# Splitting a chunk's output products by halves of the array's rows, and giving them a slot and banks of their own

## The chip, the cores and the metric

The kernel runs on one core of one Trainium2 chip. The metric is device time in microseconds (us), the median over runs of the whole program, from launch to the last store. Engines are named as in the profile: PE is the matrix engine (PEld its weight loads), DVE the vector engine, ACT the scalar engine, POOL the general one, and SP issues most DMAs.

## What is computed

A gated linear attention (a recurrence over 768 tokens, 4 batches, 8 heads of 48), whose output, laid side by side over the heads, goes through a feed-forward block of 384 to 2048 to 384 with SiLU:

```python
for t in range(S):                       # attention, state is 48 x 48 per head
    state = alpha[:, :, t, :, None] * state + einsum('bhd,bhe->bhde', k[:, :, t], v[:, :, t])
    y[:, :, t] = einsum('bhd,bhde->bhe', q[:, :, t], state)
x = y.transpose(0, 2, 1, 3).reshape(B * S, H * D)          # 3072 x 384
h = x @ w_in                                               # 384 x 2048
out = (h / (1 + exp(-h))) @ w_out                          # 2048 x 384
```

All of it is in 32-bit floats.

## The kernel before

**Chunks.** The tokens are cut into 24 chunks of C = 128 (chunk n is tokens of batch n % 4; CH = 64 is half a chunk). With scaled keys `kp` and queries `qp` (one tile holds four pairs of heads, a pair's two heads in rows 0 to 47 and 64 to 111), a chunk's attention is three kinds of product on PE:

- `scores`: keys times queries, a 128 x 128 matrix per head, of which the part with key after query is zero. ACT copies it from the accumulator banks (`ps_a`) to the tile `g`, and POOL's `affine_select` clears the wrong triangle.
- `values`: y, the chunk's output, is the sum of what comes from inside the chunk (`vn` times `g`, 16 products) and what comes from earlier chunks (the state `st` times `qp`, 12 products). Each fills 32 columns of the array, so four stand side by side (4 x 32 columns), and streams 128 tokens. All sum up in one bank, `py`; one ACT copy brings it to `xt`, the input of the feed-forward block.
- `states`: 16 products of 48 tokens add the chunk's keys and values to the state (DVE adds them).

From the ninth chunk on (n >= NA = 8) the scores of a chunk are already made in quarters (64 x 64), and the tokens of heads 4 to 7 stand with their two halves swapped, in `kp`, in `g` and in `v` alike, so that the four quarters of the array are busy at once.

**Feed-forward.** For groups of four chunks it runs as fast matrix multiplication (fewer products, more sums on DVE): `enter` makes the hidden layer (`ps_m`, 128 x 256 products), `leave` the output (`ps_o`, 128 x 192 products). Both are cut into pieces of some 2.6 us of PE time; a table of due times (`fill`) puts pieces between the attention's stages.

**Order.** `for step in range(5, STEPS)` has four slots a step. From step 8 on: slot 0 `land` and `scores` of the chunk before, slot 1 `products` (DVE: decays and `kp`), slot 2 `quotient` (DVE: `p`, then `qp`), slot 3 `values`, `states` and `flip` of the chunk before; after each slot `fill` runs the pieces that are due. On PE, the order is kept as written; on DVE, ACT and POOL a scheduler orders what is not marked (`settled`, `keep_in_program_order`), but once built the order of every engine is fixed, and each engine runs its queue strictly in that order. `least` is a chunk's total decay; ACT multiplies the state by it at the end of `scores`.

The pool `ps_a` has three banks, given out in rotation: two to `scores`, one to `values`, one to `states`.

Of the kernel before, what the change touches and what calls it, by code (L numbers as in the profile page):

```python
# [14 lines left out]
ALU = mybir.AluOpType  # L15
# [341 lines left out]
def quotients(  # L357
# [19 lines left out]
    nc = tc.nc  # L377
    dve, act, gps = nc.vector, nc.scalar, nc.gpsimd

    late = {}  # L380
# [7 lines left out]
    def settled(ins):  # L388

        return tc.keep_in_program_order(ins) if stated[0] else ins  # L390
# [55 lines left out]
    def ps_attn(n=C):  # L446
        return ps_a.tile([128, 512], F32, name="ps_a").rearrange("p (j c) -> p j c", c=n)
# [67 lines left out]
    def load_v(n):  # L515
        c = ctxs.setdefault(n, dict(zip(("ci", "b"), divmod(n, B))))
        x = v[c["b"], :, c["ci"] * C : c["ci"] * C + C, :].transpose([1, 0, 2])
        t = c["v"] = vns[n % NV]
        if n < NA:
            settled(nc.sync.dma_start(t[:, :, 0:D], x))  # L520
            return
        nc.sync.dma_start(t[:, 0 : H // 2, 0:D], x[:, 0 : H // 2])
        for e in range(2):
            nc.sync.dma_start(t[CH * e : CH * e + CH, H // 2 :, 0:D], x[CH - CH * e : C - CH * e, H // 2 :])

    wide = moe_w_in.dtype != F32
    pieces_in = [(t, c) for c in range(0, DF, 512) for t in range(NKT)]
# [238 lines left out]
    def products(n):  # L766

        if "ps" not in ctxs[n]:
            bring(n)
        c = ctxs[n]  # L770
        sg = seg[0 if late else n % 2]
        ps = c.pop("ps")
        end = NP * W
        u = upool.tile([128, end + 1], F32, name="u")
        settled(dve.tensor_tensor_scan(u[:, end - 1 :: -1], sg[:, end:0:-1], one[:, end:0:-1],  # L775
                                       0.0, ALU.mult, ALU.add))

        settled(dve.tensor_single_scalar(least[:, n, :], u[:, 0:end:W], 2.0**-64, ALU.max))  # L778
        kp = c["kp"] = turns(kps, n) if n < NA else kps[0]
        ut = tokens(u)  # L780
        if n >= NA:
            ps["k"] = late["turn"].tile([128, NP, C], F32, name="turn")
            turned(c["k"], ps["k"])
            load(n + 1, "k")
        if n < NA:
            settled(dve.tensor_tensor(kp, ps["k"], ut, ALU.mult))  # L786
            quotient(n, sg, ps["q"])
            return
        j = NP // 2
        dve.tensor_tensor(kp[:, 0:j], ps["k"][:, 0:j], ut[:, 0:j], ALU.mult)  # L790
        k, ut = [x[:, j:].rearrange("p j (e c) -> p j e c", e=2) for x in (ps["k"], ut)]
        dve.tensor_tensor(kp[:, j:].rearrange("p j (e c) -> p j e c", e=2)[:, :, ::-1], k, ut, ALU.mult)
        c["sg"] = sg

    def quotient(n, sg=None, q=None):
# [38 lines left out]
    def scores(n):  # L834
        c = ctxs[n]
        ci, b = c["ci"], c["b"]
        ps = [ps_attn() for _ in range(2)]

        for j in (0, 2, 1, 3):
            for e in range(2 if n >= NA else 1):
                for u in range(2):
                    r = slice(64 * u, 64 * u + D)
                    at = slice(CH * e, CH * e + CH) if n >= NA else slice(0, C)
                    t = slice(CH * (e ^ j // 2) if n >= NA else 0, C)
                    pe.matmul(ps[u][at, j, t], lhsT=c["kp"][r, j, at], rhs=c["qp"][r, j, t],
                              start=True, stop=True)
        if n == 1:

            room = gpool.tile([128, 4, 2, TB], F32, name="g").rearrange("p a b n -> p (a b n)")
            c["room"] = room[:, 2 * NP * C :]
        g = (room[:, 0 : 2 * NP * C] if n == 1 else decayed).rearrange(
            "p (u j c) -> p u j c", u=2, j=NP)
        swapped = decayed.rearrange("p (o u j c) -> p o u j c", o=2, u=2, j=NP // 2)
        c["g"] = (lambda u, j: g[:, u, j, :]) if n < NA else (
            lambda u, j: swapped[:, j // 2, u, j % 2, :])
        for u in range(2 if n < NA else 0):
            settled(act.copy(g[:, u], ps[u]))  # L859
            gps.affine_select(g[:, u], g[:, u], pattern=[[0, NP], [1, C]], compare_op=ALU.is_ge,  # L860
                              fill=0.0, base=0, channel_multiplier=-1)
        if n >= NA:
            ps = [x.rearrange("p (o j) c -> p o j c", o=2) for x in ps]
            for u in range(2):
                act.copy(swapped[:, :, u, :, CH:], ps[u][:, :, :, CH:])  # L865
            for r, o in earlier:
                for u in range(2):
                    act.copy(swapped[r, o, u, :, 0:CH], ps[u][r, o, :, 0:CH])
# [7 lines left out]
        if ci > 0:  # L876
            s = st[b].rearrange("p j u e -> p j (u e)")
            for j in range(NP):
                mul = act.mul(s[:, j], s[:, j], least[:, n, j : j + 1])
                if late or n == 6:  # L880
                    tc.keep_in_program_order(mul)

# [15 lines left out]
    def values(n):  # L898

        c = ctxs[n]  # L900
        ci, b, g, qp = c["ci"], c["b"], c.pop("g"), c["qp"]
        vn = c["v"].rearrange("p (j u) d -> p j (u d)", u=2)
        s = st[b].rearrange("p j u e -> p j (u e)")
        py = ps_attn()
        todo = [(3 * j + i, vn[:, j, at : at + 32], g(u, j))
                for j in range(NP) for i, at, u in ((0, 0, 0), (1, 32, 0), (2, 80, 1))]
        todo += [(3 * j + 1, vn[:, j, 48:80], g(1, j)) for j in range(NP)]
        if ci == 0:
            at = (0, 32, 48, 80)
            todo = [(3 * j + (i + 1) // 2, vn[:, j, at[i] : at[i] + 32], g(i // 2, j))  # L910
                    for j, i in ((0, 0), (0, 1), (2, 0), (1, 0), (1, 1), (3, 0), (3, 1), (2, 1),
                                 (0, 3), (0, 2), (1, 2), (3, 3), (1, 3), (2, 3), (2, 2), (3, 2))]
        if ci > 0:
            todo += [(3 * j + i, s[:, j, 32 * i : 32 * i + 32], qp[:, j, :])
                     for j in range(NP) for i in range(3)]
        for i, (at, w, x) in enumerate(todo):
            t, at = divmod(at, 4)
            pe.matmul(py[32 * at : 32 * at + 32, t, :], lhsT=w, rhs=x, start=(i < 4),
                      stop=(i >= len(todo) - 4), skip_group_check=True)
        half, e = divmod(n, 2)  # L920
        if e == 0:
            xts[half] = xtp.tile([128, NKT, TB], F32, name="xt")
        settled(act.copy(xts[half][:, :, e * C : (e + 1) * C], py[:, 0:NKT]))  # L923
    def states(n):
        c = ctxs.pop(n)
        ci, b, vn = c["ci"], c["b"], c["v"]
# [322 lines left out]
    def go_on():  # L1249

        nonlocal done
        next(pieces[done][0], None)
        done += 1
# [34 lines left out]
    def start():  # L1288
# [64 lines left out]
        stated.pop()  # L1353
        stated.append(False)

    start()
    for step in range(5, STEPS):
        stages = [[(scores, 1)], [(products, 0)], [(values, 1)], [(states, 1)]]
        if step < NA:
            stages = stages[0:2] + [stages[2] + stages[3], []]  # L1360
        elif step >= NA:
            stages = [[(land, 1), (scores, 1)], [(products, 0)], [(quotient, 0)],
                      [(values, 1), (states, 1), (flip, 0)]]
        for slot, group in enumerate(stages):
            for stage, lag in group:
                n = step - lag
                if not 0 <= n < NT:
# [8 lines left out]
            if step * SLOTS + slot == (NA + 1) * SLOTS - 1:  # L1376
                x = decayed.rearrange("p (o i c) -> p o i c", o=2, c=C)
                for r, o in later:
                    gps.memset(x[r, o, :, 0:CH], 0.0)
# [85 lines left out]
```

## Time and profile before

| what | number |
| --- | --- |
| median of 3 runs | 550.11 us (549.88 to 550.41) |
| the profiled execution's own time | 549.8 us |
| its span, first to last instruction | 548.1 us |
| PE busy / PEld / DVE / ACT / POOL | 98% / 90% / 79% / 39% / 14% of the span |
| share of the chain that ended last | PE 96%, of it `ps_m` 45%, `ps_o` 38%, `ps_a` 14% (two lines of code) |
| clock granted to PE | 0.999 of full |

How to read it: a 32-bit product of the code shows as two MATMUL rows of the trace (and two LDWEIGHTS rows), so the 16 + 12 + 16 products of `values` and `states` are 88 rows. MATMUL rows overlap: a row lasts from its start until its result is written, and the next one starts long before that. What counts is the distance between starts. `128*32` in a row is the part of the array in use, rows by columns; `128x128` is what it streams. In the rows of DVE, too, the next one starts some 0.08 us before the last has ended.

### The profile page before, as it was taken

What the parts mean: (1) busy time and instruction counts of PE and PEld (TensorE: products, weight loads), DVE (VectorE), ACT (ScalarE), POOL (GpSimd) and SP (SyncE); (2) the same over time, 40 slices, a digit from 0 to 9 for tenths busy, and PEclk for the clock granted to TensorE, in tenths of its full rate; (3) what the DMA queues carried; (4) which work ended last, traced back from release to release, by engine and by line L of the source; (5) the groups of instructions that cost most, each with busy time, mean ns of one, the idle gap of its engine ahead of it and who ended that gap; (6) DMA issues with size and microseconds to landing.
All of it is one profiled execution on the core that took longest, in us unless ns stands there. A gap on an engine that the chain in (4) does not pass through costs nothing.

```text
span 548.1 us, 12704 instructions
## 1 busy us (share of the span) xinstructions
PE 538.7 (98%) x5069; PEld 493.1 (90%) x5069; DVE 432.8 (79%) x753; ACT 216.3 (39%) x490; POOL 79.4 (14%) x146
## 2 busy tenths in 40 slices
PE   8899999999999999999999999999999999999996
PEld 8788888998999899899999999998998999999996
DVE  5999789986979799996998986998884796944421
ACT  3655554223333334444444354253264342432200
POOL 4111001131212201111121021021121000001000
PEclk9999999999999999999999999999999999999999
DMA  9999861355445434445455653716742144500001
GB/s 213 301 203 248 220 188 33 94 147 139 111 120 134 122 84 119 122 138 159 123 132 146 186 134 98 212 28 167 192 126 85 54 129 148 166 9 19 12 22 35
DMA packets 99219, 70.12 MB, mean 128 GB/s; under 512 B 56272, under 2 KB 88656, under 8 KB 99152
## 3 DMA queue, kind: packets, MB, share of 16 engines
q1 hardware_dynamic: 97232, 65.30, 46.0%
q0 software_dynamic: 1920, 3.93, 2.1%
q8 instruction: 41, 0.67, 0.5%
q14 instruction: 26, 0.21, 0.1%
HBM read 61.34 MB, written 7.86 MB: 126 GB/s over the span
## 4 chain that ended last, share of the span: by engine, by line
PE 96%; DVE 1%; issue 1%; POOL 0%; ACT 0%; DVEq 0%; ACTq 0%; POOLq 0%
PE ps_m L395 45%; PE ps_o L395 38%; PE ps_a L395 12%; PE ps_a L399 2%; DVE p L805 0%; DVE u L775 0%; PE ps_o L399 0%; POOL g L860 0%; DVE p L812 0%; DVE kp L786 0%; ACT xt L923 0%; ACT g L859 0%; ACT al L764 0%; DVE least L778 0%; ACT o L1130 0%
## 5 line engine op out<-in xcount | busy, mean ns | idle before, releaser
L395 PE MATMUL ps_o<-w_out,g 128*128 128x192 f32 x720 | 125.6, 328 | 0.0
L395 PEld LDWEIGHTS ps_o<-w_out,g 128*128 128x128 f32 x720 | 117.8, 190 | 2.7 <-issue 0.4
L395 PE MATMUL ps_m<-xt,w_in 128*128 128x256 f32 x480 | 111.6, 381 | 0.5 <-ACT xt L923 0.5
L395 PEld LDWEIGHTS ps_m<-xt,w_in 128*128 128x128 f32 x480 | 89.9, 190 | 12.7 <-ACT xt L923 0.8
L395 PE MATMUL ps_o<-wt,g 128*128 128x192 f32 x528 | 91.4, 326 | 0.0
L395 PEld LDWEIGHTS ps_o<-wt,g 128*128 128x128 f32 x528 | 87.3, 190 | 1.7 <-DVE o L1132 0.3
L395 PE MATMUL ps_m<-xc,w_in 128*128 128x256 f32 x288 | 70.6, 381 | 0.0
L1123 DVE TENSOR_TENSOR g<-g 128x512 f32<-128x512 f32 x72 | 49.6, 702 | 14.6 <-PE ps_o L395 12.2
L872 POOL TENSOR_SCALAR_AFFINE_SELECT g<-g 64x256 f32<-64x256 f32 x64 | 36.0, 563 | 165.3 <-ACT g L865 162.1
L395 PEld LDWEIGHTS ps_m<-xc,w_in 128*128 128x128 f32 x288 | 53.7, 190 | 6.7
L1015 ACT ACTIVATE g<-g 128x1024 f32<-128x1024 f32 x32 | 33.2, 1057 | 55.5 <-DVE g L1018 55.5
L1010 ACT COPY g<-ps_m 128x512 f32<-128x512 f32 x64 | 37.0, 587 | 36.7 <-PE ps_m L395 36.6
L395 PE MATMUL ps_m<-xc,wx 128*128 128x256 f32 x192 | 50.1, 383 | 0.0
L1135 POOL DMA_DIRECT2D out_dram<-o x40 | 22.1, 552 | 169.9 <-ACT o L1130 74.9
L1018 DVE TENSOR_TENSOR g<-ps_m,g 128x512 f32<-128x512 f32 x56 | 37.5, 684 | 10.9 <-PE ps_m L395 10.5
L395 PEld LDWEIGHTS ps_m<-xc,wx 128*128 128x128 f32 x192 | 35.2, 190 | 4.1 <-issue 0.4
L775 DVE TENSOR_TENSOR_SCAN u<-al,one 128x516 f32<-128x516 f32 x24 | 29.7, 1236 | 7.0 <-ACT al L764 6.6
L983 ACT ACTIVATE g<-ps_m 128x512 f32<-128x512 f32 x32 | 19.0, 597 | 33.2 <-PE ps_m L395 32.9
L805 DVE TENSOR_TENSOR_SCAN p<-al,inv 128x516 f32<-128x516 f32 x24 | 29.8, 1243 | 2.0 <-PE ps_a L395 1.1
L728 DVE TENSOR_REDUCE seen<-bits 128x1 f32<-128x512 int32 (+1 forms) x33 | 26.2, 820 | 6.0 <-DMA bits<-in_moe_w_in_dram 6.0
L1010 ACT COPY part<-ps_m 128x512 f32<-128x512 f32 x32 | 18.9, 590 | 30.4 <-PE ps_m L395 20.4
L1132 DVE TENSOR_TENSOR o<-ps_o,u 128x192 f32<-128x192 f32 x21 | 7.4, 353 | 26.9 <-PE ps_o L395 11.8
(142 smaller groups left out, 681.4 us busy)
## 6 DMA issues: line engine op xcount, KB each, us to landing
bits<-in_moe_w_in_dram SPq DMA_DIRECT2D x24, 512.0 KB, 5.1
bits<-in_moe_w_out_dram SPq DMA_DIRECT2D x16, 384.0 KB, 3.9
at<-in_alpha_dram SPq DMA_DIRECT2D x64, 96.0 KB, 2.6
kt<-in_k_dram SPq DMA_DIRECT2D x64, 96.0 KB, 2.7
qt<-in_q_dram SPq DMA_DIRECT2D x64, 96.0 KB, 2.8
bits<-in_alpha_dram SPq DMA_DIRECT2D x9, 512.0 KB, 4.0
out_dram<-o POOLq DMA_DIRECT2D x40, 96.0 KB, 2.2
flips<-turn SPq DMA_DIRECT2D x12, 256.0 KB, 2.4
```

What stands on the lines that cost most here:

```text
L395: in_order(nc.tensor.matmul(*args, **kw))
L399: in_order(nc.tensor.transpose(*args))
L728: dve.tensor_reduce(seen[kind][which][:, i : i + 1], x, axis=AX, op=op, apply_absolute_value=True))
L775: settled(dve.tensor_tensor_scan(u[:, end - 1 :: -1], sg[:, end:0:-1], one[:, end:0:-1], 0.0, ALU.mult, ALU.add))
L805: settled(dve.tensor_tensor_scan(p[:, 0:end], sg[:, 0:end], iv[:, 0:end], 0.0, ALU.mult, ALU.add))
L872: gps.affine_select(x, x, pattern=[[0, NP], [1, CH]], compare_op=ALU.is_ge, fill=0.0, base=0, channel_multiplier=-1)
L983: settled(act.activation(gts[grp, h, pair][:, i : i + 2, q % 2, :], ps, AF.Silu))
L1010: act.copy(to, ps)
L1015: return act.activation(x, x, AF.Silu)
L1018: dve.tensor_tensor(to, a, b, op)
L1123: dve.tensor_tensor(cells(grp, h, pair, *to), cells(grp, h, pair, *x), cells(grp, h, pair, *y), ALU.subtract)
L1135: (gps if grp < NG - 1 else nc.sync).dma_start(out[r : r + C, c * HO : (c + 1) * HO], o)
```

## The change

It is in the chunks from the ninth on.

- Swapped halves: instead of heads 4 to 7, the heads of every odd pair are swapped (2, 3, 6, 7). `load_v` needs six DMAs a chunk for that in place of three; `products` writes `kp` in two instructions as before, by even and odd pairs.
- y goes to three banks of `ps_a` (one for each 128 of its 384 rows), with accumulation flags of their own for each block of 32.
- `outer`, the state's share of y, is taken out of `values` and runs in slot 2, a slot sooner. Four of its products use all 128 rows of the array; the other eight, which touch one head each, use 64 rows, so that eight tiles of 64 x 32 stand side by side.
- `inner`, the chunk's own share, stays in slot 3. The later 64 tokens see all keys: 16 products of 128 rows, 64 tokens. The earlier 64 tokens see only the first 64 keys: 16 products of 64 rows and 64 tokens, eight side by side. In place of 28 products of 128 tokens a chunk has 44.
- `decay`, the state's multiplication by `least`, goes from the end of `scores` to slot 2, after `outer` of the chunk before and `quotient`.
- ACT copies y in three pieces (128 x 128) in place of one, and copies one column of a bank after `outer`.
- `apart`: one feed-forward piece is taken ahead and stands between `inner` and `states`.
- Two POOL memsets of `g` fall away.

```diff
-        nc.sync.dma_start(t[:, 0 : H // 2, 0:D], x[:, 0 : H // 2])
-        for e in range(2):
-            nc.sync.dma_start(t[CH * e : CH * e + CH, H // 2 :, 0:D], x[CH - CH * e : C - CH * e, H // 2 :])
+        to, x = [y.rearrange("p (j o u) d -> p o j u d", o=2, u=2) for y in (t[:, :, 0:D], x)]
+        for j in range(NP // 2):
+            nc.sync.dma_start(to[:, 0, j], x[:, 0, j])
+            for e in range(2):
+                nc.sync.dma_start(to[CH * e : CH * e + CH, 1, j], x[CH - CH * e : C - CH * e, 1, j])
...
+    def decay(n):
+        s = st[ctxs[n]["b"]].rearrange("p j u e -> p j (u e)")
+        for j in range(NP):
+            mul = act.mul(s[:, j], s[:, j], least[:, n, j : j + 1])
...
+    def add_y(n, j, i, half, w, x, t):
+        c = ctxs[n]
+        bank, at = divmod(3 * j + i, 4)
+        r = (low, high, slice(0, C))[half]
+        pe.matmul(c["y"][bank][32 * at : 32 * at + 32, t], lhsT=w[r], rhs=x[r, t],
+                  start=(j, i) not in c["begun"], stop=True, skip_group_check=True)
+        c["begun"].add((j, i))
+
+    def outer(n):
+        c = ctxs[n]
+        c["y"], c["begun"] = [ps_attn()[:, 0] for _ in range(NKT)], set()
+        s = st[c["b"]].rearrange("p j u e -> p j (u e)")
+        def add(j, i, half):
+            add_y(n, j, i, half, s[:, j, 32 * i : 32 * i + 32], c["qp"][:, j, :], slice(0, C))
+        for j in range(NP):
+            add(j, 1, 2)
+        for j in range(NP):
+            add(j, 0, 0)
+            add((j + 2) % NP, 2, 1)
+        act.copy(table, c["y"][1][:, 0:1])
+
+    def inner(n):
+        c = ctxs[n]
+        g, vn = c.pop("g"), c["v"].rearrange("p (j u) d -> p j (u d)", u=2)
+        def add(j, i, u, half, t):
+            at = (0, 32 + 16 * u, 80)[i]
+            add_y(n, j, i, half, vn[:, j, at : at + 32], g(u, j), t)
+        parts = ((0, 0), (1, 0), (2, 1)), ((1, 1),)
+        for part in parts:
+            for j in range(NP):
+                for i, u in part:
+                    add(j, i, u, 2, high)
+        for even, odd in (((0, 0, 0), (1, 1, 0)), ((0, 1, 0), (3, 0, 0)), ((2, 0, 0), (3, 1, 0)),
+                          ((2, 1, 0), (1, 0, 0)), ((2, 2, 1), (1, 1, 1)), ((0, 1, 1), (1, 2, 1)),
+                          ((0, 2, 1), (3, 1, 1)), ((2, 1, 1), (3, 2, 1))):
+            add(*even, 0, low)
+            add(*odd, 1, low)
+        x = x_of(n)
+        for t in range(NKT):
+            act.copy(x[:, t], c["y"][t])
...
+    def apart(n):
+        at = work_at[done]
+        while done < len(pieces) and pieces[done][2] <= bridged and work_at[done] == at:
+            go_on()
...
-            stages = [[(land, 1), (scores, 1)], [(products, 0)], [(quotient, 0)],
-                      [(values, 1), (states, 1), (flip, 0)]]
+            stages = [[(land, 1), (scores, 1)], [(products, 0)],
+                      [(outer, 1), (quotient, 0), (decay, 0)],
+                      [(values, 1), (apart, 1), (states, 1), (flip, 0)]]
```

The order on the engines moves at three places. Line numbers are those of each kernel: L739, L790, L792, L812, L1106 and L1123 of before are L741, L791, L793, L813, L1168 and L1185 after.

PE, the end of chunk 9 (counted from 0): `vn` times `g` and `st` times `p` are y, `vn` times `kn` are the states, `p` times `kp` the next chunk's scores, `ps_m` and `ps_o` feed-forward pieces. Before:

```order
L395 MATMUL ps_m<-xt,w_in 128x256 x6
L395 MATMUL ps_o<-wt,g 128x192 x8
L395 MATMUL ps_a<-g,vn_142 32x128 x16
L395 MATMUL ps_a<-p_166,st_178 32x128 x12
L395 MATMUL ps_a<-vn_142,kn 32x48 x16
L395 MATMUL ps_m<-xt,w_in 128x256 x6
L395 MATMUL ps_a<-p,kp_164 64x128 x2
```

And now:

```order
L395 MATMUL ps_m<-xt,w_in 128x256 x6
L395 MATMUL ps_a<-p_166,st_178 32x128 x12
L395 MATMUL ps_o<-wt,g 128x192 x8
L395 MATMUL ps_a<-g,vn_142 32x64 x32
L395 MATMUL ps_m<-xt,w_in 128x256 x6
L395 MATMUL ps_a<-vn_142,kn 32x48 x16
L395 MATMUL ps_a<-p,kp_164 64x128 x2
```

Small products stood at two places of a chunk, and now stand at three: the state's share alone, the chunk's own share alone, and the states with the next scores right behind them.

DVE, the query product of chunk 9 (L812, later L813: it writes `p`, which that chunk's scores read). `turn` is the transposed keys or queries; L1106 (L1168) and L1123 (L1185) are sums and differences inside `g`, the feed-forward's hidden layer. Before:

```order
L739 STREAM_TRANSPOSE turn<-kt 128x4x4x32
L790 TENSOR_TENSOR kp_164<-turn,u 128x256
L792 TENSOR_TENSOR kp_164<-turn,u 128x2x2x64
L739 STREAM_TRANSPOSE turn<-qt 128x4x4x32
L812 TENSOR_TENSOR p_166<-turn,p_166 128x4x128
L1106 TENSOR_TENSOR g<-g 128x2x2x128
```

And now:

```order
L741 STREAM_TRANSPOSE turn<-kt 128x4x4x32
L1185 TENSOR_TENSOR g<-g 128x2x2x128
L791 TENSOR_TENSOR kp_164<-turn,u 128x2x128
L793 TENSOR_TENSOR kp_164<-turn,u 128x2x2x64
L1185 TENSOR_TENSOR g<-g 128x2x2x128
L741 STREAM_TRANSPOSE turn<-qt 128x4x4x32
L605 TENSOR_TENSOR wx<-w_in 128x256
L813 TENSOR_TENSOR p_166<-turn,p_166 128x4x128
```

The two differences of `leave` (L1185) now stand ahead of the query product. They overwrite the `g` that the piece `ps_o<-w_out,g x8` reads, the piece that `apart` put between `inner` and `states` of chunk 8.

DVE, the query product of chunk 12, where a group of four chunks ends and the sums `xc` over its y (`xt`) are made for the next `enter`. Before:

```order
L739 STREAM_TRANSPOSE turn<-kt 128x4x4x32
L790 TENSOR_TENSOR kp_164<-turn,u 128x256
L792 TENSOR_TENSOR kp_164<-turn,u 128x2x2x64
L601 TENSOR_TENSOR xc<-xt 128x256 x2
L739 STREAM_TRANSPOSE turn<-qt 128x4x4x32
L1106 TENSOR_TENSOR g<-g 128x2x2x128
L812 TENSOR_TENSOR p<-turn,p 128x4x128
```

And now:

```order
L603 TENSOR_TENSOR xc<-xt 128x256
L741 STREAM_TRANSPOSE turn<-kt 128x4x4x32
L603 TENSOR_TENSOR xc<-xt,xc 128x256
L791 TENSOR_TENSOR kp_164<-turn,u 128x2x128
L793 TENSOR_TENSOR kp_164<-turn,u 128x2x2x64
L603 TENSOR_TENSOR xc<-xt 128x256 x2
L741 STREAM_TRANSPOSE turn<-qt 128x4x4x32
L608 SCALAR_TENSOR_TENSOR xc<-xt,xc 128x256
L813 TENSOR_TENSOR p<-turn,p 128x4x128
```

The sums over `xt`, which wait for the copy of y, now begin ahead of the transposed keys, and five of them stand ahead of the query product.

More of the change, by code (lines that the diff above doesn't have):

```diff
@@ L788, in products @@
             return
[L789 to L792, printed above, removed]
+        dve.tensor_tensor(kp[:, 0::2], ps["k"][:, 0::2], ut[:, 0::2], ALU.mult)
+        k, ut = [x[:, 1::2].rearrange("p j (e c) -> p j e c", e=2) for x in (ps["k"], ut)]
+        dve.tensor_tensor(kp[:, 1::2].rearrange("p j (e c) -> p j e c", e=2)[:, :, ::-1], k, ut, ALU.mult)
         c["sg"] = sg
@@ L837, in scores @@
         ps = [ps_attn() for _ in range(2)]
-        for j in (0, 2, 1, 3):
+        for j in range(NP):
             for e in range(2 if n >= NA else 1):
@@ L845, in scores @@
                     at = slice(CH * e, CH * e + CH) if n >= NA else slice(0, C)
[L846 removed]
+                    t = slice(CH * (e ^ j % 2) if n >= NA else 0, C)
                     pe.matmul(ps[u][at, j, t], lhsT=c["kp"][r, j, at], rhs=c["qp"][r, j, t],
@@ L856, in scores @@
         c["g"] = (lambda u, j: g[:, u, j, :]) if n < NA else (
-            lambda u, j: swapped[:, j // 2, u, j % 2, :])
+            lambda u, j: swapped[:, j % 2, u, j // 2, :])
         for u in range(2 if n < NA else 0):
@@ L862, in scores @@
         if n >= NA:
-            ps = [x.rearrange("p (o j) c -> p o j c", o=2) for x in ps]
+            ps = [x.rearrange("p (j o) c -> p o j c", o=2) for x in ps]
             for u in range(2):
@@ L875, in scores @@
             back(n)
[L876 to L881, printed above, removed]
+        if 0 < ci and n < NA:
+            decay(n)
+    def decay(n):
+        s = st[ctxs[n]["b"]].rearrange("p j u e -> p j (u e)")
+        for j in range(NP):
+            mul = act.mul(s[:, j], s[:, j], least[:, n, j : j + 1])
+            if late or n == 6:
+                tc.keep_in_program_order(mul)
     def back(n):
@@ L900, in values @@
         c = ctxs[n]
+        if n >= NA:
+            return inner(n)
         ci, b, g, qp = c["ci"], c["b"], c.pop("g"), c["qp"]
@@ L919, in values, with x_of @@
                       stop=(i >= len(todo) - 4), skip_group_check=True)
+        settled(act.copy(x_of(n), py[:, 0:NKT]))
+    def x_of(n):
         half, e = divmod(n, 2)
@@ L922, in values @@
             xts[half] = xtp.tile([128, NKT, TB], F32, name="xt")
-        settled(act.copy(xts[half][:, :, e * C : (e + 1) * C], py[:, 0:NKT]))
+        return xts[half][:, :, e * C : (e + 1) * C]
+    def add_y(n, j, i, half, w, x, t):
[25 more added lines that the diff above has]
+        for part in parts:
+            for j in range(NP):
+                for i, u in part:
[8 more added lines that the diff above has]
+            act.copy(x[:, t], c["y"][t])
     def states(n):
@@ L1366, in quotients @@
                 n = step - lag
-                if not 0 <= n < NT:
+                if not 0 <= n < NT or n < NA and stage in (outer, decay, apart):
                     continue
@@ L1375, in quotients @@
                     load_v(n + NV)
[L1376 to L1379, printed above, removed]
             fill(step, slot)
```

## The prediction

> **What bounds the kernel now.** I read the page's busy times first, then its chain, then the chain in order of time over one step, then PE's timeline inside one burst of small products.
>
> ```profile
> PE 538.7 (98%) x5069; PEld 493.1 (90%) x5069; DVE 432.8 (79%) x753; ACT 216.3 (39%) x490; POOL 79.4 (14%) x146
> PEclk9999999999999999999999999999999999999999
> PE 96%; DVE 1%; issue 1%; POOL 0%; ACT 0%; DVEq 0%; ACTq 0%; POOLq 0%
> ```
>
> PE carries the chain at full clock, so every 0.1 us added to PE's queue is 0.1 us of time. The chain over the step that ends chunk 12 (start, us, what):
>
> ```profile
> 204.01 2.01 PE ps_a L395 x88
> 206.02 2.79 PE ps_m L395 x12
> 208.81 0.81 PE ps_a L395 x24
> 209.63 2.81 PE ps_o L395 x16
> 212.44 2.59 PE ps_m L395 x12
> 215.03 2.60 PE ps_o L395 x16
> ...
> 224.75 2.01 PE ps_a L395 x88
> ```
>
> A step is 20.7 us without a gap. The piece behind a burst of small products takes 2.79 or 2.81 us, the same piece elsewhere 2.59 or 2.60: **leaving a burst costs 0.20**. PE's rows of the burst (start, us from first start to last end):
>
> ```profile
> 203.94 1.08 PE L395 MATMUL ps_a<-g,vn 128*32 128x128 f32 x32
> 204.84 0.84 PE L395 MATMUL ps_a<-p,st 128*32 128x128 f32 x24
> 205.50 0.52 PE L395 MATMUL ps_a<-vn,kn 128*32 128x48 f32 x32
> ...
> 205.95 1.13 PE L395 MATMUL ps_m<-xc,wx 128*128 128x256 f32 x4
> ```
>
> From 204.84 to 205.50 are 24 rows, four side by side, six rounds: 0.109 a round of 128 tokens. The 32 rows of 48 tokens are eight rounds; the last of them starts at 205.82 (below), which makes 0.043 a round. So a round is some 0.0025 plus 0.00083 a token, and one of 64 tokens, which the trace lacks, 0.056 (estimate between these two rows). Entering costs too:
>
> ```profile
> 203.69 0.33 PE L395 MATMUL ps_o<-wt,g 128*128 128x192 f32 x1
> 203.94 0.32 PE L395 MATMUL ps_a<-g,vn 128*32 128x128 f32 x4
> ...
> 205.82 0.21 PE L395 MATMUL ps_a<-vn,kn 128*32 128x48 f32 x1
> 205.95 0.48 PE L395 MATMUL ps_m<-xc,wx 128*128 128x256 f32 x1
> ```
>
> A piece of 2.60 has 16 rows of 192, 0.162 each, so the first row here is through at 203.85: 0.09 of nothing, and then 0.03 for the first weights of 32 columns (a quarter of the 0.11 that is left of the 0.20 on leaving): **0.12 to enter**. On leaving, the last row is through at 205.86, again 0.09 earlier. The four starts of a round lie within 0.02 (0.32 for all four against 0.30 for one), 7 ns apart.
>
> Is it a switch between sizes as such, or only to and from the full array? Rows where only the array's rows change, and where one small size follows another:
>
> ```profile
> 77.21 0.28 PE L395 MATMUL ps_a<-p,kp 48*128 48x128 f32 x2
> 77.42 0.33 PE L399 MATMUL ps_a<-ident,kp 128*128 128x128 f32 x1
> ...
> 15.36 0.27 PE L395 MATMUL ps_a<-p,kp 48*128 48x128 f32 x1
> 15.56 0.32 PE L395 MATMUL ps_a<-g,vn 128*32 128x128 f32 x4
> ```
>
> Rows of 128 tokens take 0.109, so the gaps are 77.42 − 77.32 and 15.56 − 15.47: 0.09 to 0.10 both times. Every switch of size costs that.
>
> **The change, part by part.**
>
> *Streaming.* Before, y takes 28 products, 56 rows, 14 rounds of 0.109: 1.53 us. Now `outer` has two rounds of 128 rows and two of eight 64-row tiles (4 × 0.109 = 0.44), `inner` eight and four rounds of 64 tokens (12 × 0.056 = 0.67). That saves **0.42** a chunk. Eight tiles at once the trace doesn't show; four of 64 x 64 it does, and there row halves run together:
>
> ```profile
> 208.74 0.33 PE L395 MATMUL ps_a<-p,kp 48*64 48x128 f32 x4
> ```
>
> The cost of the 64-row rounds lies between one turn and two; I take one, since both halves start within this row's 0.02.
>
> *Switches.* Before, a chunk's first burst costs 0.12 + 0.20, and the scores their own. Now `outer` enters (0.12), changes to 64 rows (0.12) and leaves (0.20); `inner` does the same; the states enter (0.12) and the scores follow them at no more than they paid before. That is 1.00 against 0.32: **+0.68** for 12 chunks. The last four have no states: 0.88 − 0.32 = **+0.56**. The last tile of a group starts 0.02 late with four tiles, 7 × 7 ns = 0.05 with eight: 0.16 now against 0.02, **+0.14** (+0.12 in the last four).
> PE's queue thus grows by 12 × (0.68 + 0.14 − 0.42) + 4 × (0.56 + 0.12 − 0.42) = **5.8 us**.
>
> The page "TensorEngine Tiling (Array Packing)" of the Trainium skill, section Key Properties, says that changing the tiling mode drains the array, while another tile of the same mode does not. The four switches above agree with it; by it the switch from 128 to 64 rows inside `outer` and `inner`, which no row shows with 32 columns, costs a drain too, and without it the sum would be 16 × 2 × 0.12 = 3.9 us less.
>
> *The scores' wait for DVE.* DVE is strict in order, and its new order puts work that waits for late things ahead of the query product. Durations (mean ns after the busy time):
>
> ```profile
> L1123 DVE TENSOR_TENSOR g<-g 128x512 f32<-128x512 f32 x72 | 49.6, 702 | 14.6 <-PE ps_o L395 12.2 <-PE ps_m L395 2.3
> L739 DVE STREAM_TRANSPOSE turn<-qt 128x512 f32<-128x512 f32 x16 | 17.9, 1118 | 0.3
> L601 DVE TENSOR_TENSOR xc<-xt 128x256 f32<-128x256 f32 x12 | 4.7, 415 | 0.1
> L812 DVE TENSOR_TENSOR p<-turn,p 128x512 f32<-128x512 f32 x16 | 11.0, 688 | 0.3
> L790 DVE TENSOR_TENSOR kp<-turn,u 128x256 f32<-128x256 f32 x16 | 6.9, 433 | 0.5
> L868 ACT COPY g<-ps_a 64x128 f32<-64x128 f32 x64 | 13.7, 265 | 0.4
> ...
> 346.98 1.27 DVE L1018 TENSOR_TENSOR g<-ps_m,g 128x512 f32<-128x512 f32 x2
> ```
>
> Two of 0.68 take 1.27: neighbours overlap by 0.08. Before, the product was long done:
>
> ```profile
> 130.48 0.69 DVE L812 TENSOR_TENSOR p<-turn,p 128x512 f32<-128x512 f32 x1
> 138.72 0.33 PE L395 MATMUL ps_a<-p,kp 48*64 48x128 f32 x4
> ...
> 183.89 0.68 DVE L812 TENSOR_TENSOR p<-turn,p 128x512 f32<-128x512 f32 x1
> 187.35 0.33 PE L395 MATMUL ps_a<-p,kp 48*64 48x128 f32 x4
> ```
>
> Slack was 7.5 us at chunk 9 and 2.8 at chunk 12. Now, at chunk 9, the second difference waits until the piece ahead of the states has read `g`. From that moment (plus some 0.1 to notice) DVE needs 0.70 + 1.12 + 0.42 + 0.69 − 3 × 0.08 = 2.7; PE needs only 0.12 + 0.34 + 0.09 for the states and the switch. Wait: 2.8 − 0.55 = **2.2**. At chunk 12 the first `xc` waits for the copies of y, three of some 0.26 on ACT (the nearest row, L868, is of 128 elements too), 0.6 behind `inner`. Then come seven operations of 0.42, two transposes of 1.12 and the product: with nine overlaps some 5.1, so ready 5.7 behind `inner`. PE has a piece (2.8) and the states (0.55): wait **2.4**. At chunk 11 an output sum that waits for the same kind of piece stands ahead of the product: 0.35 + 0.69 + 0.1 − 0.08 − 0.55 = **0.5**. At chunk 20, keys' and queries' transposes, two 0.70 sums, `kp` and one `xc` all stand between DVE's position when `inner` ends and the product's end, 4.9 in all against 3.4 on PE: **1.4**, the least certain, since it hangs on how far DVE then is behind. Chunk 10 about 0.1; elsewhere I find slack. Sum **6.6**; ends: 0 if DVE comes earlier than I lay it out, 9 if chunk 13 and others wait too.
>
> *The rest, taken at nothing.* ACT: three copies of y and one of a column, at most 0.265 each, in place of one of 0.474; and the DMAs of `v`:
>
> ```profile
> L923 ACT COPY xt<-ps_a 128x384 f32<-128x384 f32 x24 | 11.4, 474 | 18.3 <-PE ps_a L395 18.1
> vn<-in_v_dram SPq DMA_DIRECT2D x32, 48.0 KB, 2.9
> ```
>
> That is 4 × 0.265 − 0.474 = 0.6 a chunk, 9 us on an engine 61% idle. The column's copy holds the multiplications of the state and SiLUs queued behind it until `outer` is through; if one SiLU a group came late, up to 1 us in all, in the range. States wait for a bank until y's first copy, 0.3 to 0.4, under a piece of 2.6; if that cover went, 0.4 a chunk. `outer` takes all three banks, but the scores' copies are some 10 us old then. Three more DMAs a chunk go through SP ahead of the flips' and later loads; they land in 2.9 of a 20.7 us step. POOL's two memsets cost no path.
>
> Sum: 549.8 (profiled execution) + 5.8 + 6.6 = 562.2; the median stood 0.3 above that execution, so **562.4**.
>
> **Rivals.**
> 1. *The waits don't come* (DVE early): for it the 7.5 us of slack, against it the order. 562.4 − 6.6 = 555.8. Chance 0.12.
> 2. *Only the rows change, and that is free* with equal columns: 558.5. Against it 77.42. Chance 0.08.
> 3. *The split doesn't do what it says*: the two halves take turns in eight tiles. 16 × (2 × 0.109 + 4 × 0.056) = 7.0 more, 569.4. Against it the row at 208.74, where four tiles do not. Chance 0.09.
> 4. *Faster*: the 0.09 of a switch is the handing over of a bank and not the size, and y's own banks remove it. Nine switches a chunk, eight in the last four, 140 × 0.095 = 13.3 less: 549.1. It decides below 0.01 a switch. Against it: the gap is the same at 77.42 and 15.56, where neighbours write other banks already. Chance 0.03.
> 5. *A floor on starts.* If starts couldn't lie closer than in y's rounds before (0.109 / 4 = 27 ns on the mean), `inner`'s 64 rows would take 1.73 for 0.67 and `outer`'s 24 0.65 for 0.44: 16 × 1.27 = 20 more, 583. Against it the 48-token rows at 205.50, one every 11 ns. Chance 0.02. The page "TensorE: Matmul & The Clock Gate" of the Trainium skill (section "Wait — 56ns, not 53.3ns?") states a floor of about 25 ns from start to start however short the product; by it the same sum gives 580, but this trace contradicts it for tiles side by side.
>
> **The numbers.** Forecast 0.64, its own range 559.5 to 565.5 (waits 4 to 9, SiLUs 1); 0.02 for more. From rival 1's upper half to most of rival 3, 555 to 568, lies 0.8. Within 0.2% (1.1 us, about what can be told from no change) 0.01, faster 0.03, slower 0.96.
>
> **What would show it.** In the profile after: the chain with three `ps_a` bursts a step, each piece behind one at 2.8; inside y's bursts a gap near 0.12 where 128 rows become 64; 64-token rounds of 0.056 and eight starts within 0.05; PE idle behind DVE's query product (L813) at chunks 9, 12, 20 and 11, near 141, 194, 366 and 175 us (the scores' times before plus what has come on by then), 6 to 7 us in all, and hardly elsewhere. I am wrong if those waits are missing, or if the eight tiles start in two turns.

## The result, and the profile after

The changed kernel took **566.25 us** (565.69 to 566.84) against 550.0 before (549.65 to 550.41): 1.0295 of the time, 95% interval 1.0278 to 1.0313. The forecast was 562.4, its range 555 to 568; the likeliest case's own range ended at 565.5. The profiled execution is the one of 565.69, 15.9 more than before's 549.8; the sums below are made against it. Times are medians of all executions of a kernel; one execution of `wide_in_waits` (706.69 us) and one of `one_burst` (1434.49) stand far apart from the others, and without them the medians given below for these two would be 562.14 and 547.79.

The page of the kernel after: busy times, granted clock in 40 slices, shares of the chain that ended last.

```profile
PE 546.8 (97%) x5581; PEld 487.0 (86%) x5581; DVE 431.8 (77%) x753; ACT 218.6 (39%) x538; POOL 75.3 (13%) x144
PEclk9999999999999999999999999999999999999998
PE 82%; DVE 11%; DMA 2%; issue 2%; ACT 1%; POOL 0%; DVEq 0%; ACTq 0%; POOLq 0%
```

DVE has 11% of the chain where it had 1%. The slices of 14 us show a full clock, which hides what comes below. What PE waited for, from 120 to 450 us (us in total, times, the longest):

```profile
PE ps_a L395 <- DVE p L813: 5.9, 5, 2.3
PE ps_a L395 <- DMA kn<-flips: 0.8, 1, 0.8
PE ps_o L395 <- ACT g L1077: 0.3, 1, 0.3
PE ps_m L395 <- ACT xt L927: 0.3, 1, 0.3
```

The first line is the forecast's wait for the query product; 6.6 was laid out for it. The last one stands in before, too. A step without a wait, in the chain in order of time:

```profile
214.05 0.97 PE ps_a L395 x64
215.02 2.79 PE ps_m L395 x12
217.80 1.29 PE ps_a L395 x56
219.10 2.81 PE ps_o L395 x16
...
229.69 0.74 PE ps_a L395 x24
230.43 2.80 PE ps_o L395 x16
```

Three bursts a step: the chunk's share of y (64 rows), the states with the next scores (24 and 32), the state's share of y (24). The pieces behind them take 2.79, 2.81 and 2.80. Inside the bursts, PE's rows around the change from 128 to 64 rows (each line covers a short window and is named by its first row: the second holds the four last rows of 128 and the four first of 64):

```profile
229.62 0.32 PE L395 MATMUL ps_a<-p,st 128*32 128x128 f32 x4
229.75 0.54 PE L395 MATMUL ps_a<-p,st 128*32 128x128 f32 x8
229.98 0.45 PE L395 MATMUL ps_a<-p,st 64*32 64x128 f32 x16
235.46 0.36 PE L395 MATMUL ps_a<-g,vn 64*32 64x64 f32 x19
```

The second 128-row round starts at 229.75 and streams to 229.86 or so; its last tile, 0.02 later, to 229.88; the first 64-row product starts at 229.98. That is the 0.09 to 0.10 of the switches in before, and it is there in all 32 places (16 chunks, `outer` and `inner`).

Where the 15.9 us are: the start of each chunk's scores on PE, in both kernels.

| scores of chunk | before | after | later by | grown by |
| --- | --- | --- | --- | --- |
| 8 | 125.12 | 125.34 | 0.22 | |
| 9 | 138.72 | 141.62 | 2.90 | 2.67 |
| 10 | 154.93 | 158.58 | 3.65 | 0.76 |
| 11 | 171.14 | 175.90 | 4.76 | 1.10 |
| 12 | 187.35 | 194.82 | 7.47 | 2.71 |
| 13 | 208.74 | 218.21 | 9.47 | 2.00 |
| 14 | 229.49 | 239.12 | 9.63 | 0.16 |
| 19 | 334.75 | 346.85 | 12.09 | 0.37 a chunk, at chunk 16 0.98 |
| 20 | 355.47 | 369.12 | 13.64 | 1.55 |
| 23 | 417.91 | 432.70 | 14.79 | 0.23, 0.81, 0.11 |
| last copy of `o` starts | 543.31 | 558.33 | 15.02 | 0.23 |
| end of the span | 548.1 | 564.0 | 15.9 | 0.9 |

A chunk in which PE waits for nothing grows by 0.37; what lies above that is a wait, but for chunk 13. Between the scores of chunk 12 and 13, 1.63 too much went by without a wait. PE's rows there:

```profile
194.82 1.33 PE L395 MATMUL ps_a<-p,kp 48*64 48x128 f32 x32 [2.27 <-DVE p L813]
196.08 3.19 PE L395 MATMUL ps_m<-xc,w_in 128*128 128x256 f32 x8
199.11 1.03 PE L395 MATMUL ps_m<-xc,wx 128*128 128x256 f32 x4
```

The scores take 1.26 to the next piece where 0.83 to 0.89 is usual, and its first eight products 3.03 where eight of 0.216 take 1.73. The busy times by stretches tell why (us; busy time of PE, PEld, DVE, ACT, POOL; then the **granted clock**, the DMA share and GB/s):

```profile
194.80:196.00 1.20, 1.18 (x32) 1.12 (x32) 1.20 (x4) 0.00 (x0) 0.00 (x0) 0.64 0.71 184
196.00:200.20 4.20, 4.20 (x19) 3.49 (x15) 4.17 (x10) 2.58 (x9) 1.91 (x4) 0.70 0.42 82
200.20:210.00 9.80, 9.80 (x75) 8.71 (x74) 9.58 (x18) 4.18 (x12) 0.56 (x1) 1.00 0.38 108
```

Behind the longest wait PE ran for some 3.4 us at half its clock (its products start 0.427 apart, twice 0.216). That cost 1.63 us beyond the wait, and nothing in the forecast stood for it.

### The profile page after: what moved, and what is told of

Read it like the earlier page. It is cut to its first block, busy times and chain, and to the rows that moved or that the text cites. A ratio compares the mean times of both kernels' runs of the same rounds, so it can differ in the third digit from the quotient of the medians.

```text
span 564.0 us, 13867 instructions
## 1 busy us (share of the span) xinstructions
PE 546.8 (97%) x5581; PEld 487.0 (86%) x5581; DVE 431.8 (77%) x753; ACT 218.6 (39%) x538; POOL 75.3 (13%) x144
## 4 chain that ended last, share of the span: by engine, by line
PE 82%; DVE 11%; DMA 2%; issue 2%; ACT 1%; POOL 0%; DVEq 0%; ACTq 0%; POOLq 0%
PE ps_m L395 38%; PE ps_o L395 33%; PE ps_a L395 9%; DVE turn L741 2%; DMA bits<-in_moe_w_in_dram 2%; PE ps_a L399 1%; DVE p L813 1%; DVE u L777 1%; DVE seen L730 1%; DVE p L806 1%; DVE g L1080 1%; DVE g L1185 1%; DVE w_out L679 1%; DVE w_out L680 0%; DVE xc L603 0%
## 5 line engine op out<-in xcount | busy, mean ns | idle before, releaser
L395 PE MATMUL ps_m<-xc,w_in 128*128 128x256 f32 x288 | 72.4, 388 | 0.0
L1185 DVE TENSOR_TENSOR g<-g 128x512 f32<-128x512 f32 x72 | 48.7, 689 | 27.1 <-PE ps_o L395 24.7
L873 POOL TENSOR_SCALAR_AFFINE_SELECT g<-g 64x256 f32<-64x256 f32 x64 | 33.5, 524 | 179.1 <-ACT g L866 164.7
L395 PE MATMUL ps_a<-p,kp 48*64 48x64 f32 (+2 forms) x640 | 24.1, 260 | 6.2 <-DVE p L813 6.2
```

Of the source, the lines that this page charges most:

```text
L395: in_order(nc.tensor.matmul(*args, **kw))
L873: gps.affine_select(x, x, pattern=[[0, NP], [1, CH]], compare_op=ALU.is_ge, fill=0.0, base=0, channel_multiplier=-1)
L1185: dve.tensor_tensor(cells(grp, h, pair, *to), cells(grp, h, pair, *x), cells(grp, h, pair, *y), ALU.subtract)
```

## The experiments

All ratios are to before on the same chip (549.3 to 549.5 us there).

**DVE's order alone.** `query_first`: in a step's last slot, and in chunk 12 in the pieces of the slot before, DVE gets nothing ahead of the query product.

```diff
+        ready[n] = settled(dve.tensor_tensor(qp, q, qp, ALU.mult)).ins
...
+          with tc.issue_after(ready[step]) if slot == 3 and NA < step < NT else nullcontext():
             for stage, lag in group:
...
+            with tc.issue_after(ready[step]) if slot >= 2 and NA < step < NT and (slot == 3 or step == 12) else nullcontext():
+                fill(step, slot)
```

> DVE's order alone is changed: in the last slot of a step (in chunk 12 from the slot before) nothing may stand ahead of that chunk's query product. PE's order stays. Theory (of the 16 us, 5.6 are the waits for the query product at chunks 9 to 12, and the half clock behind the longest of them is another 1.6 to 2.7): 566.25 - 5.6 - 2 = 558.6, with PE waiting under 0.3 us at chunks 9 to 12 and a granted clock of 1.00 everywhere after 10 us. Rival A (the work put behind the query product is then late itself and PE waits for that): 563 to 566, with waits of ps_m or ps_o pieces for DVE or ACT in place. Rival B (the half clock is not due to the wait): 560.5, with the slow piece still there.

Measured: 559.41 us, 1.0183 (1.0166 to 1.0200), by the ratios some 6 us less than after. PE's longest waits from 120 to 450 us:

```profile
PE ps_a L395 <- DMA kn<-flips: 0.8, 1, 0.8
PE ps_a L395 <- DVE p L815: 0.6, 2, 0.3
PE ps_a L395 <- ACT xt L986: 0.4, 1, 0.4
```

And the busy times of the stretch around chunk 12's scores, with the granted clock (1.00):

```profile
185.00:205.00 20.00, 20.00 (x243) 17.84 (x243) 18.30 (x38) 9.80 (x27) 2.48 (x5) 1.00 0.38 100
```

The waits for the product fell from 5.9 to 0.6 us. From chunk 12 to 13 the growth is 0.37, the clock full. Chunks 9, 11, 12, 13 grow by 0.37 each, chunk 10 by 0.77. So the order cost the waits, and the half clock went with them. Of 7.6 us expected 7.0 show at chunks 9 to 13; 0.9 came back as waits of a few tenths that are new at chunks 14 and 22, a little of rival A.

**Is it the idle time that halves the clock?** `busy_in_waits` and `wide_in_waits` are after, with PE kept busy ahead of the scores of chunks 9 and 12 by products whose sums are thrown away, so the scores start no sooner.

```diff
+        if n in (9, 12):
+            for _ in range(6):      # busy_in_waits: 96 products of 48 tokens
+                for i in range(16):
+                    pe.matmul(ps[0][32 * (i % 4) : 32 * (i % 4) + 32, 0, 0:D], lhsT=ident[:, 0:32],
+                              rhs=ident[:, 0:D], start=True, stop=True)
...
+            for _ in range(9):      # wide_in_waits: 9 of 128 x 128
+                pe.matmul(ps[0][:, 0, :], lhsT=ident, rhs=ident, start=True, stop=True)
```

> Ahead of the scores of chunks 9 and 12, 96 small products (some 2.0 us of PE's time, their sums thrown away) run while PE would wait for the query product. Theory (the 2.4 us wait at chunk 12 lowers PE's clock, and this is 1.2 us behind chunk 12's scores and 0.4 in them): the waits shrink to some 0.4 us each, the scores start no earlier, but the piece behind chunk 12's scores takes 2.80 us instead of 4.02 and the scores 0.89 instead of 1.29, at a granted clock of 1.00 in that stretch. Rival (that piece is slow for a reason of its own, say its operands xc, which DVE writes just then): 4.0 us again, at a clock of 0.7. The total is not a clean measure, since the added products also move the vector engine's order further on; by the theory it lies 1.6 us or more below 566.25, so at 564.6 or less; by the rival at 566.

Measured: 565.84 us, 1.0294 (1.0261 to 1.0327), and not the test it was meant to be. PE's rows at chunk 12:

```profile
193.07 1.96 PE L395 MATMUL ps_a<-ident 128*32 128x48 f32 x166
197.35 0.53 PE L395 MATMUL ps_a<-ident 128*32 128x48 f32 x26 [2.32 <-issue]
```

After 166 of the 192 rows PE stood still for 2.3 us with nothing to wait for, and the piece behind was slow again. The idle time was not removed but only got another cause, so theory and rival both allow it. Hence the second:

> As busy_in_waits, whose many small products came to a stop of 2.3 us in the middle, with nothing that they waited for, so that PE was idle again and the piece was slow again (427 ns a product): now nine products of 128 x 128, 0.22 us each, stand ahead of the scores of chunks 9 and 12. Theory (2.4 us of idle PE halve its clock, whatever it waits for): with the idle time at chunk 12 under 0.7 us, the piece behind its scores takes 2.8 us and the scores 0.89. Rival (the piece is slow for a reason of its own): 4.0 us again, at half clock.

Measured: 562.76 us, 1.0246 (1.0227 to 1.0265). PE's rows there:

```profile
192.15 2.27 PE L395 MATMUL ps_a<-ident 128*128 128x128 f32 x18
194.43 0.90 PE L395 MATMUL ps_a<-p,kp 48*64 48x128 f32 x32
195.26 1.99 PE L395 MATMUL ps_m<-xc,w_in 128*128 128x256 f32 x8
```

And the stretch of the scores and the piece behind them:

```profile
194.40:200.00 5.60, 5.59 (x58) 5.18 (x58) 5.57 (x13) 3.04 (x9) 2.07 (x4) 1.00 0.46 104
```

The scores are as late as in after (chunk 12 grows by 2.65, there by 2.71), but from 12 to 13 the growth is 0.37 instead of 2.00: same order of the pieces, same wait for DVE, full clock. So it is the idle PE that costs the clock, and the rival falls. (This is the profiled execution, 561.88; one of the others took 563.38 at a mean clock of 0.994, so the clock may have fallen somewhere there, but no trace of it was kept.)

**The same kernel three times**, since the wait at chunk 9 is as long as that at chunk 12 and left the clock alone:

> The changed kernel once more, unchanged, for one look at where its clock falls. Theory (the waits of 2.3 us at chunk 9 and 2.4 at chunk 12 are both long enough, and whether the clock is halved behind one hangs on when in the execution it falls): the stretch of half clock stands behind chunk 9, behind chunk 12, behind both or behind neither, another way in another execution; each costs 1.2 to 1.7 us, so spans from 562.4 to 565.5. Rival (only chunk 12's is long enough, or its piece is special): behind chunk 12 and never behind chunk 9, in each execution, with a span of 564.0 to 564.4.

> As after_again_1: theory, half clock behind chunk 9, 12, both or neither, and not the same in each execution; rival, behind chunk 12 alone in each.

> As after_again_1: theory, half clock behind chunk 9, 12, both or neither, and not the same in each execution; rival, behind chunk 12 alone in each.

Measured: 564.88, 567.19 and 565.16 us, one execution each. In the second the clock fell behind both waits (the growth from chunk 9 to 10 is 2.40 there and 0.76 or 0.77 in the others, 1.64 for the fall), in the other two and in the profiled one only behind chunk 12. So the same program's clock can fall or not behind the same wait, and the rival is out.

What decides can be read from the clock records of the traces. Every fall lasts 3.41 us and begins a whole number of such windows after the trace's first clock record. So each execution has a grid of windows, and the grid lies at another place of the program each time. Cut by this grid, the windows that hold the wait at chunk 9, and the one that holds the wait at chunk 12 with the one behind it, in the profiled execution of after (busy times and granted clock as above):

```profile
137.10:140.51 3.41, 2.28 (x44) 1.92 (x42) 2.87 (x6) 0.30 (x1) 0.00 (x0) 1.00 0.01 3
140.51:143.92 3.41, 2.30 (x39) 2.09 (x40) 3.40 (x9) 1.26 (x6) 0.51 (x1) 1.00 0.50 125
...
191.71:195.12 3.41, 1.14 (x50) 0.81 (x52) 3.41 (x9) 0.30 (x1) 0.00 (x0) 1.00 0.49 128
195.12:198.53 3.41, 3.41 (x35) 2.80 (x27) 3.41 (x8) 1.73 (x7) 1.39 (x3) 0.50 0.58 131
```

And the window with the wait at chunk 9 in the second of the three, with the one behind it:

```profile
139.17:142.58 3.41, 1.18 (x64) 1.07 (x64) 3.41 (x7) 0.30 (x1) 0.00 (x0) 1.00 0.13 35
142.59:146.00 3.41, 3.41 (x20) 2.66 (x11) 3.32 (x8) 1.39 (x6) 1.67 (x4) 0.50 0.47 114
```

Where the wait at chunk 9 lay across two windows, in three of the four executions, PE was busy for 1.9 us or more of each, and the clock stayed. Where a wait lay within one window, at chunk 12 in all four and at chunk 9 in one, PE was busy for 1.1 to 1.2 of the 3.41 us, and the next window ran at half clock. The stop of 2.3 us in `busy_in_waits` is the sixth such case. In all twelve traces, up to 540 us, no other window had less than 1.78 us of busy PE, and no other fall stands behind one. Where between 1.2 and 1.8 the limit lies no run shows.

**The split by halves.** `whole_rows` is `query_first` with y's 28 products of before at the places of after, and with POOL's two memsets of `g` back:

```diff
         for j in range(NP):
-            add(j, 1, 2)
-        for j in range(NP):
-            add(j, 0, 0)
-            add((j + 2) % NP, 2, 1)
+            for i in range(3):
+                add(j, i, 2)
...
-                    add(j, i, u, 2, high)
-        for even, odd in (((0, 0, 0), (1, 1, 0)), ((0, 1, 0), (3, 0, 0)), ((2, 0, 0), (3, 1, 0)),
...
+                    add(j, i, u, 2, slice(0, C))
```

> As query_first, but y is not split by halves of the rows: 28 products of 128 rows and 128 tokens as before the change, at the places of after (state's share in slot 2, chunk's share in slot 3, banks of its own). Theory (the prediction's: the split saves 0.42 us of streaming a chunk and pays 2 x 0.12 for two changes from 128 to 64 rows and 0.14 for the later ends): within 1 us of query_first, some 0.04 x 16 = 0.6 above it. Rival A (a change of rows alone is free): 16 x 0.28 = 4.5 above it. Rival B (eight tiles take turns): 16 x 0.44 = 7 below it.

Measured: 561.71 us, 1.0229 (1.0212 to 1.0246), 2.3 above `query_first`. A chunk without a wait grows by 0.47 instead of 0.37, in the chain 0.80 and 1.01 for the two bursts of y against 0.73 and 0.97. So the split is worth 0.10 a chunk, 1.6 us in all, where the forecast's terms gave 0.04 (by this difference the later ends cost 0.08, not 0.14). The rest is 0.6 us that this profiled execution took longer up to chunk 8, where the two kernels are alike, and waits that came and went: 0.9 came at chunk 18, 0.4 to 0.5 went at each of chunks 14 and 22. Rival A and B are both out: by them the difference would be 4.5 or −7.

**The number of bursts.** `y_at_once` is `whole_rows` with the state's share of y in slot 3 and without ACT's copy of one column; `states_with_y` further drops `apart`, writes the states to free columns of y's third bank, in y's burst, and copies y behind them:

```diff
-                      [(outer, 1), (quotient, 0), (decay, 0)],
-                      [(values, 1), (apart, 1), (states, 1), (flip, 0)]]
+                      [(quotient, 0), (decay, 0)],
+                      [(outer, 1), (values, 1), (apart, 1), (states, 1), (flip, 0)]]   # y_at_once
...
+                      [(outer, 1), (values, 1), (states, 1), (bring_y, 1), (flip, 0)]]  # states_with_y
...
+            ps = ps_attn() if n < NA else c["banks"][2][:, 1:3].rearrange("p a (b d) -> p (a b) d", b=2)
```

> As whole_rows, but the state's share of y runs in slot 3 right ahead of the chunk's share: one burst less a chunk. Theory (entering a burst costs 0.12 and leaving it 0.20, wherever it stands): 16 x 0.32 = 5.1 us less than whole_rows. Rival (the price of a burst is hidden, or comes back as a wait for one of y's banks): less than 2 us below it.

> As y_at_once, but the piece of apart is gone and the states follow y in the same burst, written to the free columns of y's third bank: the order of PE is that of before again, with three banks for y, the odd pairs swapped and the vector engine's order of query_first. Theory (all that is left of the change's cost on PE is the states' own burst, 0.14 a chunk in y_at_once, and 2 to 4 us of waits that came with the order): 550 to 551.5, and a growth of 0.02 us a chunk or less against before. Rival (three banks or the swapped odd pairs cost by themselves): 553 or more, with a growth that stays in each chunk.

Measured: `y_at_once` 557.54 us, 1.0152 (1.0135 to 1.0169), and 0.14 a chunk instead of 0.47: a burst less is 0.33, as by the theory. Of 5.3 us 4.2 show in the time; the rest turned into waits (the longest for `kn` is 1.4 in place of 0.8, one for a SiLU 0.9 in place of 0.5). `states_with_y` 556.34 us, 1.0138 (1.0123 to 1.0154): 0.04 a chunk is left, so three banks and the swapped pairs cost PE next to nothing; but the total missed the expectation by 5 us. Its waits:

```profile
PE ps_o L395 <- DVE o L1193: 3.2, 2, 2.8
PE ps_a L395 <- DMA kn<-flips: 0.8, 1, 0.8
```

The stretch of the longest of them, and the one behind it:

```profile
389.50:392.70 3.20, 0.42 (x3) 0.02 (x1) 3.17 (x6) 0.17 (x1) 0.00 (x0) 1.00 0.03 5
392.70:394.00 1.30, 1.30 (x8) 1.30 (x9) 1.30 (x3) 0.00 (x0) 0.54 (x1) 1.00 0.45 60
```

With PE's work shifted, DVE's order has an output sum behind a query product and two reductions at 392 us, and PE waits 2.8 us. This time the clock stayed full: the wait lay across two windows of that execution's grid, in which PE was busy for 1.82 and 2.22 us.

**The other way round.** `one_burst`, from before: y, states and the next scores in one burst a chunk. The states go to the columns of the scores' banks that no quarter uses.

```diff
+            next_ps = ctxs[n + 1]["room for scores"] = [ps_attn() for _ in range(2)]
...
+                    to = ps[r, j, 0:D] if n < NA else next_ps[j // 2][r, 2 * (1 - i // 2) + j % 2, 0:D]
...
+            if n >= NA:
+                scores_pe(n + 1)
```

> Built from before, and meant to be faster than it: the other way round, one burst of small products a chunk in place of two. y (28 products in one bank, as before), the states and the next chunk's scores follow each other on PE; the states go to the columns of the scores' banks that no quarter uses; DVE's additions to the state come after ACT's copies of the scores, and DVE's order keeps the query products ahead of later work. Theory (a burst is entered for 0.12 to 0.15 and left for 0.20, a change between two small sizes costs 0.12 to 0.15): some 0.21 us a chunk less than before on PE, over 15 chunks 3.2 us, so 549.5 - 3.2 = 546.3, if the query product is ready a piece sooner everywhere. Rival (it isn't, or pieces now wait for ACT): PE waits of 1 us and more at single chunks, 549 to 552.

Measured: **547.85 us**, 0.9973 of before (0.9963 to 0.9982). The chain:

```profile
225.18 2.82 PE ps_a L395 x112
228.01 2.81 PE ps_o L395 x16
230.82 2.59 PE ps_m L395 x12
```

PE's longest wait from 120 to 450 us:

```profile
PE ps_m L395 <- DVE g L1046: 1.4, 2, 1.2
```

One burst of 2.82 and one piece of 2.81, where before has 2.01 and 0.81 with two such pieces: 0.19 to 0.21 less in each undisturbed chunk, as expected. Of these 3 us 1.3 went again between the scores of chunks 13 and 14, where PE waits for a sum of the hidden layer that stands behind two scans on DVE, and 0.8 at chunks 22 and 23. That the total is 1.5 all the same is owed to the tail: from the end of the last copy of `o` to the end of the span 0.66 less passes than before, which is not explained.

## Why the prediction was right, and where it fell short

By its own steps, against the profiled execution's 15.9 us:

| step of the prediction | forecast | measured |
| --- | --- | --- |
| PE's queue, a chunk with states | 0.40 | 0.37 (0.16 at chunk 14) |
| PE's queue, a chunk of the last four | 0.26 | 0.11 to 0.23 |
| PE's queue in all | 5.8 | 5.0 |
| wait for the query product, chunk 9 | 2.2 | 2.30 |
| chunk 10 | 0.1 | 0.39 |
| chunk 11 | 0.5 | 0.73 |
| chunk 12 | 2.4 | 2.34 |
| chunk 20 | 1.4 | 0.4 (and `kn`'s 0.8 ahead of it, counted below) |
| half clock behind a wait | – | 1.6 |
| the rest, taken at nothing | 0 | `kn` 0.8, SiLU 0.6, chunk 22 0.6, the end 0.9, the start 0.2 |

(The measured waits are a chunk's growth less 0.37. Chunk 14 grows by 0.21 less since the piece behind its new burst took 2.81 in before too, without a burst ahead of it. The 0.6 at chunk 22 is no fixed cost: in the three repeats that chunk grows by 0.23, 0.23 and 0.35. The forecast's sums come out but for roundings: 16 × 2 × 0.12 is 3.8, and 562.2 + 0.3 is 562.5.) *The two main steps held.* The bursts, the switch of rows alone, the tiles side by side and the DVE order behaved as read from before's trace. `query_first` shows the DVE order by itself, `y_at_once` a burst, `whole_rows` the split as a whole; its parts are read from the rows. All five rivals fall: the waits came; the row switch costs 0.09 to 0.10; eight tiles start 7 ns apart and a 64-token round takes 0.056; the gaps are there with y in banks of its own; no floor on starts shows.

*Mis-sized: "PE at full clock".* The forecast took the clock for granted because before shows 9 in every slice, and priced a wait at its length. At chunk 12 it was 2.3 + 1.6. That is the largest part of the 3.9 us between 562.4 and 566.25. The median lies 0.6 above the profiled execution; the one with the half clock behind both waits, 567.19, lies 1.5 above it. In all, the terms that the forecast had came to 11.2 where it laid out 12.4, and 4.7 came from what it took at nothing. That 566.25 still lies within 555 to 568 is partly luck: the upper end was set by rival 3, not by any of these.

The Trainium skill's page "TensorE: Matmul & The Clock Gate", section "What's actually happening", has the mechanism: a gate that lets half or all of the clock through, set by how busy PE was in a free-running window of some 3.4 us. The trace agrees on the half (0.427 against 0.216), on the length (3.41 us in each of the six falls) and on the free-running window: the same wait did it in one execution and not in another, by where the grid lay. It does not bear out that a whole idle window is needed: 2.2 to 2.3 us within one window did it here, with PE busy for 1.1 to 1.2 us of the window, while 2.8 us across two windows did not.

*Missed: "DMAs ... land in 2.9 of a 20.7 us step".* The keys for chunk 19's states came 0.8 late. SP's queue ahead of them:

```profile
352.55 0.54 SPq L825 DMA_DIRECT2D flips<-turn  x1
361.74 0.35 SPq L716 DMA_DIRECT2D bits<-in_moe_w_in_dram  x1
362.14 0.42 SPq L505 DMA_DIRECT2D at<-in_alpha_dram  x1
362.66 0.38 SPq L833 DMA_DIRECT2D kn<-flips  x1
```

In before the same loads were issued 12.6 us ahead of chunk 20's scores (355.47), here 6.5 (369.12):

```profile
342.90 1.80 SPq L832 DMA_DIRECT2D kn<-flips  x4
```

And DVE's row, in after, that reads the buffer:

```profile
360.44 1.27 DVE L730 TENSOR_REDUCE seen<-bits 128x1 f32<-128x512 int32 x2
```

SP issues nothing for 9 us until DVE has read the buffer that `bits` will overwrite, and the loads of `kn` queue behind it. So a late DVE reaches PE through SP's queue too, which the forecast didn't follow: it counted the DMAs added, not what the queue waits for. This is read from the order of the rows; no run took it away. That chunk 20's sum (1.18) came out near the 1.4 is partly luck, since the late `kn` hides some of the wait for the product.

*Open:* the 0.9 us at the end. From the end of the last copy of `o` (543.31 + 0.32, 558.33 + 0.32) to the end of the span 4.4 us pass before and 5.3 after, 5.3 to 5.5 in each kernel built from after, 3.8 in `one_burst`. No run was made for it.

## What to carry to other kernels

On a PE that never waits, count bursts, not products: each visit of another tile size costs 0.3 us here, and the split that saved 0.4 us of streaming was left with 0.1 after its own two switches. When code moves, follow the strict queues of the other engines to the next thing that PE needs, SP's queue too; 6 of the 16 us came from there, without an operation having become slower. And price a wait of 2 us or more on PE at more than its length: where it lies within one window of the clock's grid, another 1.6 us come on top, and where it lies the program doesn't decide.

## What the hardware showed that was not expected

- The clock granted to PE is set window by window, on a grid of 3.41 us. A window in which PE was busy for 1.1 to 1.2 us was followed by one at half clock, six times of six, at some 1.6 us lost each; a window with 1.78 us or more was not, in any of twelve traces. So 2.3 us of idle PE within one window cost the clock, and 2.8 us across two did not.
- 166 rows of small products, each with a weight load, went through in 1.96 us, and then PE stood still for 2.3 us without waiting for anything that the profile shows. Nine large products of the same total time did not stop. Both stops of `busy_in_waits` (at 195.03, and one of 1.4 us at 141.28) end 2.3 us after a packet of 16 KB began on the DMA queue that the trace calls instruction (195.03 to 197.35, 140.37 to 142.71). The Trainium skill's page "Runtime: NRT & Kernel Launch", section "Instruction fetch mechanics", says that an engine's instructions stream in by blocks and that this is mostly hidden. The times fit a wait for such a block; no run varied it alone.
